# A last layer in row-major form: residual rows by DMA transposes instead of PE transposes, with merged row phases and paired elementwise work

## The chip, the cores and the metric

One core of one Trainium2 chip. The metric is the device time of one execution in microseconds (us). The kernel before takes 478.95 us (median of 3 runs, 478.73 to 479.54). In the profile the engines are PE (TensorE matmul), PEld (its weight load), DVE (VectorE), ACT (ScalarE), POOL (GpSimd) and SP (SyncE, which here only issues DMA). The profiled span runs from the first to the last instruction and is about 1.8 us shorter than the timed execution (476.7 against 478.50 in the profiled run of before, 479.2 against 481.02 in that of the changed kernel).

## The reference

A cross network (DCN v2) with 6 layers, batch 16384, width 416, all tensors bf16:

```python
B, F, D, L = 16384, 26, 16, 6           # Din = F * D = 416
def reference(x0, ws, bs):
    x = x0
    for l in range(L):
        proj = jnp.einsum('bd,de->be', x, ws[l]) + bs[l]
        x = x0 * proj + x
    return x
```

## The kernel before

The batch is cut into 8 groups of 2048 rows; (g, l) is one layer of one group. The kernel holds x transposed: features on the 128 partitions, batch rows along the free dimension, as three blocks of 128 features plus a tail of 32. A job (g, l) has three output tiles of 128 features; each is 12 full matmuls of 512 columns and 4 small ones, then ACT adds the bias out of PSUM, and DVE multiplies by x0 and adds the old x. Jobs of different groups are interleaved, so that PE need not wait for the elementwise work:

```python
order[-6:] = [(5, 5), (7, 3), (6, 4), (7, 4), (6, 5), (7, 5)]     # the last six jobs
...
late = items.index(("tile", (LAST, L - 2), NT - 1))               # (7,4)'s last tile goes last
items.append(items.pop(late))
```

A finished group is turned back into rows by DMA transposes into a staging buffer and stored, all of it on the SP queue, which issues them in the order of the program (in the SP timeline further down at 451.73, 454.33, 456.22 and 464.19 us):

```python
def output(g):
    turn(0)                                   # DMA transpose, 128 features x 2048 rows
    add("sp", ... dma_start_transpose(ot3, x3s[s3]) ...)          # the 32-feature tail
    add("pool", ... tensor_copy(ost[..., 384:416], ot3) ...)
    turn(1); turn(2)
    ... dma_start(rows ..., ost ...)          # the store, 1664 KB
```

The very last job (7,5) is different. It computes rows directly (x as the stationary operand, W as the moving one), so that its output needs no turning at the end. For that the residual x of group 7 (the input of layer 5) must also be in rows. The kernel before turns it on PE, in two row phases that share the PSUM banks with the matmuls:

```python
def turn_main(kp, bks, ts):                   # PE transposes into PSUM
    for j in range(NJ):
        for h2 in range(2):
            for t in ts:
                add("pe", ... h.transpose(psum_t(bks[j])[...], xcol(t, j, kk), ident) ...)

def rows_out(kp, bks):                        # PSUM to SBUF, 832 columns each
    for j in range(NJ):
        eng = "act" if j == 0 or (kp and j == 2) else "dve"
        ...
def nat_mul(kk, j, b):                        # ACT copies 416 columns out of PSUM, DVE multiplies by x0
    ...
def nat_add(kk, j):                           # DVE adds the residual, 416 columns
    ...
turn_main(0, bka, (0, 1)); turn_tails(0, bka); nat_rows(0, bkb, True)
for j in range(NJ): nat_full(0, j, bkb[j], False, (0, 1))
turn_main(0, bka, (2,)); rows_out(0, bka)
layer_full(0, bkb, (2,))
turn_main(1, bka, (0, 1, 2)); turn_tails(1, bka); rows_out(1, bka)
nat_rows(1, bkb, True); layer_full(1, bkb)
nat_store(0, 2, 0, NJ)                        # stores: 832, 416, 208, 104 and 104 KB
nat_rows(2, bka, True); layer_full(2, bka); nat_store(2, 3, 2, NJ)
nat_rows(3, bkb, True); layer_full(3, bkb); nat_store(3, 4, 3, NJ, "act")
```

## Time and profile before

| | before |
|---|---|
| time, median of 3 | 478.95 us |
| span of the profile | 476.7 us |
| last column-major matmul ends | 458.0 us |
| group 6's store issues | 464.19 us |
| DVE's last add ends | 474.47 us |

The page's head and its DMA queue q1 (packets, MB, share of 16 engines' time), for the kernel before:

```profile
span 476.7 us, 8467 instructions
PE 470.2 (99%) x3403; PEld 198.7 (42%) x3403; DVE 406.9 (85%) x714; ACT 342.4 (72%) x371; POOL 7.2 (2%) x14
...
q1 hardware_dynamic: 131064, 51.20, 46.8%
...
PE 92%; SPq 4%; DVE 2%; ACT 1%; DMA 0%; issue 0%
```

The last line is the chain of waits by engine: for 92% of the span the kernel waits for PE. The change concerns only the end, where this average says nothing.

For comparing ends I use a mark: the start of the last group of 16 small 32x32 matmuls, which every kernel of this study has. In the PE timeline of before (start, duration, line, operation, count) it is the first of these lines:

```profile
447.02 0.43 PE L471 MATMUL ps<-x,w 32*32 32x512 bf16 x16
447.25 0.42 PE L488 MATMUL ps<-x,w 32*32 32x512 bf16 x8
```

So the end, from the mark, takes 476.7 - 447.02 = 29.68 us. I call this the tail. The spans are read to 0.1 us here, so a tail is good to 0.05 us.

The DVE timeline of before, its last entries:

```profile
461.69 1.57 DVE L795 COPY x<-ps 128x832 bf16<-128x832 bf16 x3
...
473.48 0.58 DVE L825 TENSOR_TENSOR x<-ps,x 128x416 bf16<-128x416 f32 x1
474.09 0.38 DVE L835 TENSOR_TENSOR x<-x,x 128x416 bf16<-128x416 bf16 x1
```

DVE runs from 461 to 474.47 us with no idle stretch over 0.2 us; the span ends 2.2 us after it, which is the last small store. The SP queue of before (when each DMA is issued):

```profile
451.73 2.20 SPq L636 DMA_TRANSPOSE ost<-x  x1
454.33 1.20 SPq L641 DMA_TRANSPOSE ot<-x  x1
456.22 4.32 SPq L636 DMA_TRANSPOSE ost<-x  x2
464.19 0.38 SPq L655 DMA_DIRECT2D out_dram<-ost  x1
468.96 4.98 SPq L842 DMA_DIRECT2D out_dram<-x  x4
```

Group 6 is turned from 451.7 us on and stored at 464.19. The same stretch as windows (start and end, length, busy time of PE, PEld, DVE, ACT and POOL in this order, granted clock, DMA share, GB/s; the DMA share is the summed time of the packets over 16 engines, so overlapping packets can bring it above 1, as in the 1.17 and 1.10 of the changed kernel further down):

```profile
458.00:465.00 7.00, 6.88 (x95) 4.80 (x93) 7.00 (x20) 4.29 (x8) 0.00 (x0) 1.00 0.85 135
465.00:473.30 8.30, 7.38 (x52) 3.85 (x49) 7.99 (x26) 6.25 (x13) 0.00 (x0) 1.00 1.00 334
473.30:476.70 3.40, 0.00 (x0) 0.00 (x0) 1.13 (x3) 0.00 (x0) 0.00 (x0) 0.97 0.54 188
```

The DMA engines are full from 465 to 473, but only 0.54 busy in the last 3.4 us: they have caught up and wait for DVE. I read from this that the end of the kernel before is DVE's; e3 below supports it.

### The profile page before, as it was taken

Reading aid. Unit: us, or ns where it says so; the run is one execution under the profiler, and the core shown is the slowest. Engines: PE = TensorE matmul, PEld = TensorE weight load, DVE = VectorE, ACT = ScalarE, POOL = GpSimd, SP = SyncE. Lnnn points to the kernel's source line nnn. Section 1 sums busy time; section 2 is a strip of 40 time slices with the busy share of each in tenths; the row PEclk is TensorE's granted clock in tenths of the full one; section 3 lists DMA queues with packets and bytes.
Section 4 is the critical chain, followed back from the end, with each engine's and each line's share of the span. In section 5 each row is a group of like instructions: output and inputs, shape, how many; then the busy total and the mean of one; then the engine's idle time right before and its main releaser. Section 6 shows DMA issues by size and latency. Waiting matters only on the chain.

```text
span 476.7 us, 8467 instructions
## 1 busy us (share of the span) xinstructions
PE 470.2 (99%) x3403; PEld 198.7 (42%) x3403; DVE 406.9 (85%) x714; ACT 342.4 (72%) x371; POOL 7.2 (2%) x14
## 2 busy tenths in 40 slices
PE   8999999999999999999999999999999999999996
PEld 6344444444444444444444444434444444444353
DVE  2888888888888888898888879888888888888897
ACT  4677777777777777777777777777777777777775
POOL 0000000000000000000000000000000000000000
PEclk9999999999999999999999999999999999999999
DMA  8886920720102477379219932970000138026388
GB/s 232 179 176 144 195 66 1 157 65 1 34 1 46 76 212 156 75 168 242 57 35 211 207 80 40 189 236 0 2 15 21 26 64 231 0 45 159 108 145 286
DMA packets 131851, 52.27 MB, mean 110 GB/s; under 512 B 108122, under 2 KB 130404, under 8 KB 131812
## 3 DMA queue, kind: packets, MB, share of 16 engines
q1 hardware_dynamic: 131064, 51.20, 46.8%
q8 instruction: 26, 0.43, 0.4%
q10 hardware_dynamic: 748, 0.54, 0.3%
q14 instruction: 13, 0.11, 0.1%
HBM read 5.97 MB, written 13.63 MB: 41 GB/s over the span
## 4 chain that ended last, share of the span: by engine, by line
PE 92%; SPq 4%; DVE 2%; ACT 1%; DMA 0%; issue 0%
PE ps L456 75%; PE ps L477 7%; PE ps L497 7%; SPq L292 2%; PE ps L800 1%; PE ps L471 1%; DVE x L408 1%; DVE tw L403 1%; SPq L297 1%; PE ps L488 1%; SPq L285 0%; SPq L521 0%; ACT tw L394 0%; PE ps L770 0%; DMA x<-ost 0%; SPq L304 0%
## 5 line engine op out<-in xcount | busy, mean ns | idle before, releaser
L394 ACT ACTIVATE tw<-ps,bias 128x1024 bf16<-128x1024 f32 (+1 forms) x295 | 299.8, 1071 | 120.0 <-PE ps L477 75.9
L456 PE MATMUL ps<-x,wm 128*128 128x512 bf16 x1692 | 379.4, 379 | 0.0
L456 PEld LDWEIGHTS ps<-x,wm 128*128 128x128 bf16 x1692 | 159.0, 98 | 213.2 <-issue 28.3
L403 DVE TENSOR_TENSOR tw<-tw,x 128x1024 bf16<-128x1024 bf16 (+1 forms) x285 | 192.7, 685 | 53.9 <-ACT tw L394 53.6
L408 DVE TENSOR_TENSOR x<-tw,x 128x1024 bf16<-128x1024 bf16 (+1 forms) x285 | 182.5, 681 | 0.0
L477 PE MATMUL ps<-x,w 32*128 32x512 bf16 x512 | 39.2, 379 | 0.2 <-DMA x<-ost 0.2
L497 PE MATMUL ps<-x,wm 128*32 128x512 bf16 x564 | 33.0, 380 | 0.0
L434 ACT ACTIVATE ts<-ps,bias 128x512 bf16<-128x512 f32 x47 | 28.8, 701 | 0.0
L438 DVE TENSOR_TENSOR x<-ts,x 128x512 bf16<-128x512 bf16 x47 | 18.6, 417 | 3.0 <-DMA x<-x 3.0
L497 PEld LDWEIGHTS ps<-x,wm 128*32 128x32 bf16 x564 | 13.8, 96 | 17.6 <-issue 5.3
L477 PEld LDWEIGHTS ps<-x,w 32*128 32x128 bf16 x512 | 7.8, 92 | 27.9 <-issue 27.1
L436 DVE TENSOR_TENSOR ts<-ts,x 128x512 bf16<-128x512 bf16 x47 | 18.6, 418 | 0.0
L643 POOL COPY ost<-ot 128x512 bf16<-128x512 bf16 x7 | 6.3, 900 | 449.9 <-DMA ot<-x 449.9
L800 PE MATMUL ps<-wm,x 128*128 128x416 bf16 x48 | 9.4, 341 | 0.0
L568 DVE COPY x<-ps 128x512 bf16<-128x512 bf16 x4 | 1.7, 425 | 8.0 <-PE ps L561 8.0
L828 ACT ACTIVATE x<-ps 128x416 bf16<-128x416 f32 x15 | 7.1, 525 | 1.3 <-PE ps L800 1.1
L565 ACT ACTIVATE x<-ps 128x512 bf16<-128x512 bf16 x8 | 4.3, 594 | 4.8 <-PE ps L561 4.8
L800 PEld LDWEIGHTS ps<-wm,x 128*128 128x128 bf16 x48 | 5.1, 115 | 3.8 <-issue 1.4
L488 PE MATMUL ps<-x,w 32*32 32x512 bf16 x188 | 5.9, 374 | 0.0
L830 DVE TENSOR_TENSOR x<-x,x 128x416 bf16<-128x416 bf16 x15 | 5.4, 368 | 0.3 <-ACT x L828 0.2
L471 PE MATMUL ps<-x,w 32*32 32x512 bf16 x208 | 5.6, 385 | 0.0
L835 DVE TENSOR_TENSOR x<-x,x 128x416 bf16<-128x416 bf16 x16 | 5.6, 369 | 0.1
(35 smaller groups left out, 43.2 us busy)
## 6 DMA issues: line engine op xcount, KB each, us to landing
out_dram<-ost SPq DMA_DIRECT2D x7, 1664.0 KB, 6.8
x<-in_x_dram SPq DMA_DIRECT2D x7, 416.0 KB, 7.1
x<-x SPq DMA_DIRECT2D x24, 96.0 KB, 2.2
wm<-in_ws_dram SPq DMA_DIRECT2D x5, 312.0 KB, 3.4
x<-x SPq DMA_DIRECT2D x22, 64.0 KB, 2.0
x<-ost SPq DMA_DIRECT2D x28, 32.0 KB, 2.3
out_dram<-x SPq DMA_DIRECT2D x1, 832.0 KB, 4.3
x<-x SPq DMA_DIRECT2D x24, 32.0 KB, 1.9
```

The lines of the kernel that those rows point to most:

```text
L394: add("act", lambda h, a=a, w=w, b0=b0: h.activation(tw[r][:, a * CH:(a + w) * CH], psum[:, b0 * CH:(b0 + w) * CH], ACT_F.Identity, bias=b ...
L403: add("dve", lambda h, a=a, e=e: h.tensor_tensor(tw[r][:, a * CH:e * CH], tw[r][:, a * CH:e * CH], x0s[s0][:, i * GC + a * CH:i * GC + e * ...
L408: add("dve", lambda h, a=a, e=e: h.tensor_tensor(xs[so][:, i * GC + a * CH:i * GC + e * CH], tw[r][:, a * CH:e * CH], src(i, a, e), ALU.ad ...
L434: add("act", lambda h: h.activation(ts[r][:, :], bank(b), ACT_F.Identity, bias=bias[:, 3, l:l + 1], scale=1.0), reads=[("ps", b), "bias"], ...
L436: add("dve", lambda h: h.tensor_tensor(ts[r][:, :], ts[r][:, :], x03, ALU.mult), reads=[("ts", r)] + tok0, writes=[("ts", r)], release=True)
L438: add("dve", lambda h: h.tensor_tensor(x3s[so][:, :], ts[r][:, :], res, ALU.add), reads=[("ts", r)] + rtok, writes=[("x3", so), ("x3", so, ...
L456: add("pe", lambda h, t=t, j=j: h.matmul(bank(banks[j]), wm[l][:, t, ecols], src(t, j, j + 1), start=(first and t == 0), stop=(not first a ...
L471: add("pe", lambda h, q=q, j=j, r=r, c=c, o=o: h.matmul(psum[o, banks[j] * CH:(banks[j] + 1) * CH], w3[l][q, i * P + c * T32:i * P + (c + ...
L477: add("pe", lambda h, q=q, j=j, r=r: h.matmul(bank(banks[j]), w3[l][q, ecols], src[q, :], start=first, stop=not first, tile_position=(r * ...
L488: add("pe", lambda h, l=l, b=b, s3=s3, ri=ri, qi=qi, ro=ro, qo=qo: h.matmul(psum[qo, b * CH:(b + 1) * CH], w3[l][qi, NT * P:D], s3[qi, :], ...
L497: add("pe", lambda h, t=t, j=j, src=src, l=l, b=b, ro=ro, qo=qo: h.matmul(psum[qo, b * CH:(b + 1) * CH], wm[l][:, t, NT * P:D], src(t, j, ...
L800: add("pe", lambda h, t=t: h.matmul(bank(b, n=D), xcol(t, j, kk), wm[l][:, t, :], start=(first and t == 0), stop=(not first and t == NT - 1)),
```

## The change

The intent is to take work off PE and DVE in the end. The residual rows come by DMA transposes; PE transposes and their copies out of PSUM go; the two first row phases are merged, since no banks are needed for transposes; DVE works on pairs of 416 columns; the bias matmuls use 32 rows (of which 31 are zero) instead of one. For the residual to be in time, group 6's last layer moves ahead of group 7's fifth. Rows now lie as blocks of 128, so each store piece is one row of 832 bytes. "Spread" is the copy that puts the turned 32-feature tail into its columns of the staged rows. The excerpt below leaves out smaller parts of the change: group 6's tail is now turned after its three blocks, the last column-major tile leaves PSUM in pairs of 512 columns, and x0's rows and the bias rows are prepared for the new forms.

```diff
-    order[-6:] = [(5, 5), (7, 3), (6, 4), (7, 4), (6, 5), (7, 5)]
   (the order is then ..., (5,5), (6,4), (7,3), (6,5), (7,4), (7,5))
-    where[((LAST - 1, L - 1), 0)] = batches[-1]
+    where[((LAST - 1, L - 1), 1)] = batches[-1]
-    late = items.index(("tile", (LAST, L - 2), NT - 1))
-    items.append(items.pop(late))
 ...
+    def rest_turn(t, j0=0, j1=NJ):                 # the residual, by DMA
+        s = xset[(LAST, L - 1)]
+        add("sp", lambda h: h.dma_start_transpose(
+            x5f[:, j0 * KK:j1 * KK, t * P:(t + 1) * P], xs[s][:, t * GC + j0 * CH:t * GC + j1 * CH]),
+            reads=..., writes=[("x5n", j, t) for j in range(j0, j1)], ...)
 ...
         finish_tile(g, l)
+        if (g, l) == (LAST, L - 2):
+            if i < NT - 1:
+                rest_turn(i)
+            else:
+                rest_turn(i, 0, 2)
+                rest_turn(i, 2, 4)
+                spread(LAST - 1, "act")            # group 6's tail columns, was on POOL
+                rest_spread()
+                store(LAST - 1)                    # group 6's store, now behind the residual
 ...
-    (turn_main, turn_tails, rows_out: gone)
+    nat_rows(first)                                # row phases 0 and 1 together
+    for t in range(NT - 1):
+        for kk, bks in first:
+            for j in range(NJ):
+                nat_full(kk, j, bks[j], False, (t,))
 ...
+        o, x5v = on[:, j:j + 2, kk, :], x5n[:, j:j + 2, kk, :]    # pairs of 416 columns
 ...
+        dst = out[LAST * GC:B, :].rearrange("(j k p) f -> p j k f", j=NJ, k=KK)[:, j0:j1, kk, :]
```

More of the change, by code (lines that the diff above doesn't have):

```diff
@@ L625, in load_last @@
         for j in range(NJ):
-            add("sp", lambda h, j=j: h.dma_start(x0n7[:, j, :, :], perm(rows7, j)),
+            add("sp", lambda h, j=j: h.dma_start(
+                x0n7[:, j, :, :], rows7[j * CH:(j + 1) * CH, :].rearrange("(k p) f -> p k f", k=KK)),
                 writes=(x0_all(sn) + x03_toks(sn) if j == 0 else []) + [("n7", j)], lane="n7", batch=0)
@@ L629, in load_last @@
             add("sp", lambda h, j=j: h.dma_start(brow[j * T32:j * T32 + 1, :], bs[L - 1:L, :]),
-                writes=[("brow", j)] + (["brow"] if j == 0 else []), lane="brow", batch=0)
+                reads=["brow"], writes=[("brow", j)], lane="brow", batch=0)
     def output(g):
@@ L638, in turn, with turn_tail, spread, copy @@
                 reads=[("x", s, t, j) for j in range(NJ)], writes=[("ost", t)], lane="ot", batch=g)
+        def turn_tail():
+            add("sp", lambda h: h.dma_start_transpose(ot3[:, :, :], x3s[s3][:, :]),
+                reads=[("x3", s3)], writes=["ot3"], lane="ot3", batch=g)
         turn(0)
-        add("sp", lambda h: h.dma_start_transpose(ot3[:, :, :], x3s[s3][:, :]),
-            reads=[("x3", s3)], writes=["ot3"], lane="ot3", batch=g)
-        add("pool", lambda h: h.tensor_copy(
-            ost[:, :, NT * P:D].rearrange("p (j k) f -> p j k f", j=NJ),
-            ot3[:, :, :].rearrange("p k (j f) -> p j k f", j=NJ)),
-            reads=["ot3"], writes=[("ost", NT)])
-        turn(1)
-        turn(2)
+        if g < LAST - 1:
+            turn_tail()
+            spread(g, "pool")
+            turn(1)
+            turn(2)
+            store(g)
+        else:
+            turn(1)
+            turn(2)
+            turn_tail()
+            rest_tail()
+        free_x.append(s)
+        free_3.append(s3)
+    def spread(g, eng):
+        dst = ost[:, :, NT * P:D].rearrange("p (j k) f -> p j k f", j=NJ)
+        sp_ = ot3[:, :, :].rearrange("p k (j f) -> p j k f", j=NJ)
+        copy(eng, dst, sp_, reads=["ot3"], writes=[("ost", NT)])
+    def copy(eng, dst, sp_, **kw):
+        if eng == "act":
+            add("act", lambda h: h.activation(dst, sp_, ACT_F.Copy), **kw)
+        else:
+            add(eng, lambda h: h.tensor_copy(dst, sp_), **kw)
+    def store(g):
         rows = out[g * GC:(g + 1) * GC, :]
@@ L658, in output, with rest_tail, rest_spread @@
                 writes=[("out", g, j0)], lane="out", batch=g)
-        free_x.append(s)
-        free_3.append(s3)
+    x5f = x0s[s5][:, 0:XW + CH].rearrange("p (a f) -> p a f", f=D)
+    hold = []
+    def rest_tail():
+        add("pool", lambda h: h.memset(warm[:, :], 0.0), writes=x0_all(s5) + x03_toks(s5) + ["x5 free"])
+        s3 = xtail[(LAST, L - 1)]
+        hold.append(free_x.pop())
+        ot5 = xs[hold[0]][:, 0:CH].rearrange("p (k f) -> p k f", k=KK)
+        add("sp", lambda h: h.dma_start_transpose(ot5, x3s[s3][:, :]),
+            reads=[("x3", s3)], writes=[("x", hold[0], 0, 0)], lane="ot5", batch=0)
+    def rest_spread():
+        n = turn_of(LAST, L - 1)
+        staged = xs[hold[0]][:, 0:CH].rearrange("p (k q f) -> p q k f", k=KK, q=NJ)
+        for j0, j1 in ((0, NJ - n), (NJ - n, NJ)):
+            if j0 < j1:
+                q0 = (j0 + n) % NJ
+                copy("act", x5n[:, j0:j1, :, NT * P:D], staged[:, q0:q0 + j1 - j0, :, :],
+                     reads=[("x", hold[0], 0, 0), "x5 free"], writes=[("x5n", j, NT) for j in range(j0, j1)])
+    def rest_turn(t, j0=0, j1=NJ):
+        s = xset[(LAST, L - 1)]
+        add("sp", lambda h: h.dma_start_transpose(
+            x5f[:, j0 * KK:j1 * KK, t * P:(t + 1) * P], xs[s][:, t * GC + j0 * CH:t * GC + j1 * CH]),
+            reads=[("x", s, t, j) for j in range(j0, j1)] + ["x5 free"],
+            writes=[("x5n", j, t) for j in range(j0, j1)], lane=f"x5_{t}{j0}", batch=0)
     items = []
     where = {(b[min(1, len(b) - 1)], 0): b for b in batches[:-1]}
-    where[((LAST - 1, L - 1), 0)] = batches[-1]
+    where[((LAST - 1, L - 1), 1)] = batches[-1]
     del where[((0, 0), 0)]
@@ L729, in bass_standalone__cross_network_dcn__recsys_kernel @@
     first_job()
+    add("pool", lambda h: h.memset(brow[:, :], 0.0), writes=["brow"])
     for n, it in enumerate(items):
@@ L740, in bass_standalone__cross_network_dcn__recsys_kernel @@
             rows32(g, l, i, banks, False, mode[n] == "F1")
-            evacuate(g, l, i, banks, list(range(NJ)), 2)
+            if (g, l, i) == (LAST, L - 2, 0):
+                evacuate(g, l, i, banks, [0, 1], 1)
+                evacuate(g, l, i, banks, [2, 3], 2)
+            else:
+                evacuate(g, l, i, banks, list(range(NJ)), 2)
         else:
@@ L745, in bass_standalone__cross_network_dcn__recsys_kernel @@
             if n == len(items) - 1:
-                full(g, l, i, banks, False, True, lambda j: evacuate(g, l, i, banks, [j], 1))
+                full(g, l, i, banks, False, True,
+                     lambda j: evacuate(g, l, i, banks, [j - 1, j], 2) if j % 2 else None)
             else:
@@ L750, in bass_standalone__cross_network_dcn__recsys_kernel @@
         finish_tile(g, l)
+        if (g, l) == (LAST, L - 2):
+            if i < NT - 1:
+                rest_turn(i)
+            else:
+                rest_turn(i, 0, 2)
[3 more added lines that the diff above has]
+                store(LAST - 1)
     g, l = LAST, L - 1
@@ L757, in xcol @@
     def xcol(t, j, kk):
-        return src(t, j, j + 1).rearrange("p (m k) -> p m k", k=KK)[:, :, kk]
+        return src(t, j, j + 1)[:, kk * P:(kk + 1) * P]
     def x3col(j, kk):
-        return s3[quad(g, l, j)[1], :].rearrange("p (m k) -> p m k", k=KK)[:, :, kk]
-    first_use = {"x5": True, "on": True}
-    def turn_main(kp, bks, ts):
-        for j in range(NJ):
-            for h2 in range(2):
-                for t in ts:
-                    o = h2 * CH + t * P
-                    add("pe", lambda h, j=j, t=t, kk=2 * kp + h2, o=o: h.transpose(
-                        psum_t(bks[j])[:, o:o + P], xcol(t, j, kk), ident[:, :]),
-                        reads=[stok(t, j), "ident"], writes=[("ps", bks[j])])
-    def turn_tails(kp, bks):
-        for h2 in range(2):
-            for j in range(NJ):
-                r, q = quad(g, l, j)
-                o = h2 * CH + NT * P
-                add("pe", lambda h, j=j, q=q, r=r, kk=2 * kp + h2, o=o: h.matmul(
-                    psum_t(bks[j])[:, o:o + T32], x3col(j, kk), ident[q, q], is_transpose=True,
-                    tile_position=(r * T32, 0)),
-                    reads=tok3 + ["ident"], writes=[("ps", bks[j])])
-    def rows_out(kp, bks):
-        for j in range(NJ):
-            extra = x0_all(s5) + x03_toks(s5) if first_use.pop("x5", None) else []
-            eng = "act" if j == 0 or (kp and j == 2) else "dve"
-            dst = x5n[:, j, 2 * kp:2 * kp + 2, :]
-            sp_ = psum_t(bks[j]).rearrange("p (a f) -> p a f", a=2)[:, :, 0:D]
-            if eng == "act":
-                add("act", lambda h, dst=dst, sp_=sp_: h.activation(dst, sp_, ACT_F.Copy),
-                    reads=[("ps", bks[j])], writes=extra + [("x5n", j, kp)])
-            else:
-                add("dve", lambda h, dst=dst, sp_=sp_: h.tensor_copy(dst, sp_),
-                    reads=[("ps", bks[j])], writes=extra + [("x5n", j, kp)])
+        return s3[quad(g, l, j)[1], kk * P:(kk + 1) * P]
+    first_use = {"on": True}
     def nat_full(kk, j, b, first, ts=range(NT)):
@@ L803, in nat_full, with nat_rows @@
                 reads=[stok(t, j), ("wm", l)], writes=[("ps", b)])
-    def nat_rows(kk, bks, first):
-        for part in range(2):
+    def nat_rows(kks):
+        for kk, bks in kks:
             for j in range(NJ):
                 r, q = quad(g, l, j)
-                st, sp_ = first and part == 0, not first and part == 1
-                if part == 0:
-                    add("pe", lambda h, j=j, q=q, r=r, st=st: h.matmul(
-                        bank(bks[j], n=D), x3col(j, kk), w3[l][q, :], start=st, stop=False,
-                        tile_position=(r * T32, 0)),
-                        reads=tok3 + [("w3", l, r)], writes=[("ps", bks[j])])
-                else:
-                    add("pe", lambda h, j=j, r=r, sp_=sp_: h.matmul(
-                        bank(bks[j], n=D), ones[r * T32:r * T32 + 1, :], brow[r * T32:r * T32 + 1, :],
-                        start=False, stop=sp_, tile_position=(r * T32, 0)),
-                        reads=["ones", ("brow", r)], writes=[("ps", bks[j])])
@@ L821, in nat_mul @@
-    def nat_mul(kk, j, b):
-        extra = x0_all(so) + x03_toks(so) if first_use.pop("on", None) else []
-        o, x0v = on[:, j, kk, :], x0n7[:, j, kk, :]
-        if kk == KK - 1 and j == NJ - 1:
-            add("dve", lambda h: h.tensor_tensor(o, bank(b, n=D), x0v, ALU.mult),
-                reads=[("ps", b), ("n7", j)], writes=extra + [("on", j, kk)])
-        else:
-            add("act", lambda h: h.activation(o, bank(b, n=D), ACT_F.Copy),
-                reads=[("ps", b)], writes=extra + [("on", j, kk)])
-            add("dve", lambda h: h.tensor_tensor(o, o, x0v, ALU.mult),
-                reads=[("on", j, kk), ("n7", j)], writes=[("on", j, kk)])
+                add("pe", lambda h, kk=kk, b=bks[j], j=j, q=q, r=r: h.matmul(
+                    bank(b, n=D), x3col(j, kk), w3[l][q, :], start=True, stop=False, tile_position=(r * T32, 0)),
+                    reads=tok3 + [("w3", l, r)], writes=[("ps", bks[j])])
@@ new lines, in nat_rows, with nat_mul @@
+        for kk, bks in kks:
+            for j in range(NJ):
+                r, q = quad(g, l, j)
+                add("pe", lambda h, b=bks[j], q=q, r=r: h.matmul(
+                    bank(b, n=D), ones[q, :], brow[q, :], start=False, stop=False, tile_position=(r * T32, 0)),
+                    reads=["ones", ("brow", r)], writes=[("ps", bks[j])])
+    def nat_mul(kk, j, bks):
+        extra = x0_all(so) + x03_toks(so) if first_use.pop("on", None) else []
+        for a in (j, j + 1):
+            add("act", lambda h, a=a: h.activation(on[:, a, kk, :], bank(bks[a], n=D), ACT_F.Copy),
+                reads=[("ps", bks[a])], writes=extra + [("on", a, kk)])
+        o, x0v = on[:, j:j + 2, kk, :], x0n7[:, j:j + 2, kk, :]
+        toks = [("on", j, kk), ("on", j + 1, kk)]
+        add("dve", lambda h: h.tensor_tensor(o, o, x0v, ALU.mult),
+            reads=toks + [("n7", j), ("n7", j + 1)], writes=toks)
@@ L833, in nat_add, with nat_store @@
     def nat_add(kk, j):
-        o, x5v = on[:, j, kk, :], x5n[:, j, kk, :]
+        o, x5v = on[:, j:j + 2, kk, :], x5n[:, j:j + 2, kk, :]
+        toks = [("on", j, kk), ("on", j + 1, kk)]
         add("dve", lambda h: h.tensor_tensor(o, o, x5v, ALU.add),
-            reads=[("on", j, kk), ("x5n", j, kk // 2)], writes=[("on", j, kk)])
+            reads=toks + [("x5n", a, t) for a in (j, j + 1) for t in range(NT + 1)], writes=toks)
     stores = [0]
-    def nat_store(k0, k1, j0, j1, eng="sp"):
-        dst = out[LAST * GC:B, :].rearrange("(j p k) f -> p j k f", j=NJ, k=KK)[:, j0:j1, k0:k1, :]
-        add(eng, lambda h: h.dma_start(dst, on[:, j0:j1, k0:k1, :]),
-            reads=[("on", j, kk) for j in range(j0, j1) for kk in range(k0, k1)],
-            writes=[("out7", k0, j0)], lane=f"out7_{stores[0]}", batch=0)
+    def nat_store(kk, j0, j1, eng="sp"):
+        dst = out[LAST * GC:B, :].rearrange("(j k p) f -> p j k f", j=NJ, k=KK)[:, j0:j1, kk, :]
+        add(eng, lambda h: h.dma_start(dst, on[:, j0:j1, kk, :]),
+            reads=[("on", j, kk) for j in range(j0, j1)],
+            writes=[("out7", kk, j0)], lane=f"out7_{stores[0]}", batch=0)
@@ L845, in nat_store @@
         stores[0] += 1
     bka, bkb = take(NJ), take(NJ)
-    last = KK - 1
-    def layer_full(kk, bks, ts=range(NT)):
-        for j in range(NJ):
-            nat_full(kk, j, bks[j], False, ts)
-            nat_mul(kk, j, bks[j])
-            if kk < last:
-                if j:
-                    nat_add(kk, j - 1)
-            elif j == 1:
-                nat_add(kk, 0)
-                nat_add(kk, 1)
-                nat_store(kk - 1, kk + 1, 0, 2)
-            elif j == 2:
-                nat_add(kk, 2)
-                nat_store(kk, kk + 1, 2, 3)
-        nat_add(kk, NJ - 1)
@@ L866, in bass_standalone__cross_network_dcn__recsys_kernel @@
-    turn_main(0, bka, (0, 1))
-    turn_tails(0, bka)
-    nat_rows(0, bkb, True)
-    for j in range(NJ):
-        nat_full(0, j, bkb[j], False, (0, 1))
-    turn_main(0, bka, (2,))
-    rows_out(0, bka)
-    layer_full(0, bkb, (2,))
-    turn_main(1, bka, (0, 1, 2))
-    turn_tails(1, bka)
-    rows_out(1, bka)
-    nat_rows(1, bkb, True)
-    layer_full(1, bkb)
-    nat_store(0, 2, 0, NJ)
-    nat_rows(2, bka, True)
-    layer_full(2, bka)
-    nat_store(2, 3, 2, NJ)
-    nat_rows(3, bkb, True)
@@ L884, in bass_standalone__cross_network_dcn__recsys_kernel @@
-    layer_full(3, bkb)
-    nat_store(3, 4, 3, NJ, "act")
+    first = [(0, bka), (1, bkb)]
+    nat_rows(first)
+    for t in range(NT - 1):
+        for kk, bks in first:
+            for j in range(NJ):
+                nat_full(kk, j, bks[j], False, (t,))
+    for js in ((0, 1), (2, 3)):
+        for kk, bks in first:
+            for j in js:
+                nat_full(kk, j, bks[j], False, (NT - 1,))
+    nat_mul(0, 0, bka)
+    nat_mul(0, 2, bka)
+    nat_mul(1, 0, bkb)
+    nat_add(0, 0)
@@ new lines, in bass_standalone__cross_network_dcn__recsys_kernel @@
+    nat_mul(1, 2, bkb)
+    nat_add(1, 0)
+    nat_add(0, 2)
+    nat_store(0, 0, NJ)
+    nat_add(1, 2)
+    nat_store(1, 0, NJ)
+    for kk, bks in ((2, bka), (3, bkb)):
+        nat_rows([(kk, bks)])
+        for j in range(NJ):
+            nat_full(kk, j, bks[j], False)
+            if j % 2:
+                nat_mul(kk, j - 1, bks)
+                nat_add(kk, j - 1)
+                if kk == KK - 1:
+                    nat_store(kk, j - 1, j + 1, "sp" if j == 1 else "act")
+        if kk < KK - 1:
+            nat_store(kk, 0, NJ)
```

## The prediction

> **What bounds it now.** Span 476.7 us, timed 478.95. The page has PE busy 99%, DVE 85%, ACT 72%; the chain of waits is 92% PE. Only the end changes. Timeline of the end: the last column-major tile leaves PE at 457.9, DVE finishes its residual add at 461.4, row-mode matmuls end about 472.2, DVE's last add at 474.47, the last store about 476.2. There PE runs 48 full matmuls at 187 ns (9.0 us), 32 small ones (2 us) and 64 transposes (about 3.0 us of issue). DVE is the closer limit: no gap over 0.2 us from 461 to 474.
>
> **Removed.** (a) 64 PE transposes: 3.0 us of PE. (b) Eight PSUM-to-SBUF copies of 832 columns: 5 on DVE (2.6 us), 3 on ACT (2.5). (c) Pairing: 31 DVE operations of 416 columns at 0.286 us net become 16 of 832; interpolated from the net times of 512 (0.335) and 1024 columns (0.62) these take 0.51 each: 9.0 to 8.2 us. (d) The GpSimd copy at 457.3, beside which a DVE add took 0.4 us longer[...].
>
> **Added.** Five DMA transposes on the SP queue: about 8 us of issue (2.2 full, 1.2 small or half). Three ACT copies (1.6 us), where ACT now waits. Stores in 832-byte pieces: the present group stores have them and reach 350 GB/s.
>
> **New schedule (estimate).** The order change puts group 6's last layer earlier; tile counts up to 457.9 are unchanged. SP issues group 6's transposes at about 446 to 455, the residual's at 456 to 463; the last land near 465 to 466. PE waits about 0.8 us at 458 for ACT to free the last tile's banks, since no transposes cover that now; matmuls end near 470.3 (before 472.2). DVE's first row-mode add comes about 466.4, just after the residual lands. From there DVE is back to back: thirteen operations, last add near 473 (before 474.5). So most of what is removed is lost to ACT's evacuation (16 copies at 0.44 us) and that late first add.
>
> **The store tail takes part back.** DMA share is about 1.0 from 465 to 473 at 350 GB/s: group 6's store and group 7's share the engines. Group 6's store still cannot issue before 463.5 (behind the residual transposes). 3.33 MB at 350 GB/s from 464.5 is 9.5 us: 474 at best; with the last 208 KB issued at 473 it lands about 475, end about 475.5. [...]
>
> **Prediction:** 477.6 us (0.3% faster), 8 in 10 between 475.8 and 479.5. Faster by over 2%: 0.01; within 2%: 0.97; slower by over 2%: 0.02.
>
> **What would show it.** Right: no PE transposes after 458, row mode ending near 470, DVE's last add near 473, DMA share about 1 from 465 to 475, the span before 450 unchanged within 0.3 us. Wrong if: DVE's first add waits beyond 467 for a transpose (each us late is nearly a us of span); or transposes land by 464 and the store goes early, so the end is 474 or less; or PE waits over 1 us for the last evacuation; or the reordered tiles wait on rotated tails around 447 to 452.
>
> **What would make it wrong.** SBUF-to-SBUF transposes queueing (about 2.4 us of DMA each at 212 GB/s), or the new order slowing the middle.

## The result, and the profile after

The changed kernel takes 480.94 us (median of 6 runs, 480.62 to 481.34) against 479.02 us before (6 runs). The ratio is 1.004, 95% interval 1.0027 to 1.0053: within 2%, and slower, not faster. A ratio here is the mean time of one kernel's fast runs over that of the other's in the same rounds, so it is not quite the ratio of the medians quoted.

The page of the changed kernel, the lines that answer to those of before:

```profile
span 479.2 us, 8276 instructions
PE 461.9 (96%) x3285; PEld 195.0 (41%) x3339; DVE 402.3 (84%) x691; ACT 341.2 (71%) x371; POOL 6.3 (1%) x15
...
q1 hardware_dynamic: 140056, 52.79, 49.1%
...
PE 91%; DVE 2%; DMA 2%; ACT 2%; issue 1%; SPq 0%; ACTq 0%; DVEq 0%
```

DVE has 4.6 us less to do and PE 8.3 us less by the page. Not all of the PE figure is real: 54 matmuls are missing from this trace (1638 of 1692 on the line of the full matmuls). The SP queue has 1.6 MB more to move: 1.7 MB of residual transposes, less 0.1 MB of stores that now go through ACT's queue. The span is 2.5 us longer. The mark:

```profile
448.06 0.43 PE L470 MATMUL ps<-x,w 32*32 32x512 bf16 x16
```

The mark is 1.04 us later than before. The tail is 479.2 - 448.06 = 31.14 us, 1.46 us more than the 29.68 of before. So the longer span has two parts: 1.04 us that were lost before the mark, and 1.46 us in the tail. From the first such group of 16 (28.09 us before, 29.13 after) to the mark it is 418.93 us in both, so the 1.04 us were lost in the first 29 us, where the two programs have the same instructions but for one memset on GpSimd.

DVE in the end:

```profile
460.93 1.28 DVE L407 TENSOR_TENSOR x<-tw,x 128x1024 bf16<-128x1024 bf16 x2
465.27 0.59 DVE L856 TENSOR_TENSOR x<-x,x 128x832 bf16<-128x832 bf16 x1 [3.06 <-ACT x L852]
...
467.42 0.59 DVE L862 TENSOR_TENSOR x<-x,x 128x832 bf16<-128x832 bf16 x1
...
473.93 0.59 DVE L862 TENSOR_TENSOR x<-x,x 128x832 bf16<-128x832 bf16 x1
```

DVE's last add ends at 474.52 us, 26.46 us after the mark, where it was 27.45 before: DVE is 0.99 us earlier. The change did that part of its work. But the span ends 4.7 us after that add, not 2.2. The SP queue of after says where to look:

```profile
446.89 7.69 SPq L636 DMA_TRANSPOSE ost<-x  x3
454.62 1.95 SPq L641 DMA_TRANSPOSE ot<-x  x1
456.61 1.26 SPq L693 DMA_TRANSPOSE x<-x  x1
457.99 8.41 SPq L707 DMA_TRANSPOSE x<-x  x4
466.50 0.53 SPq L678 DMA_DIRECT2D out_dram<-ost  x1
469.54 4.56 SPq L869 DMA_DIRECT2D out_dram<-x  x4
```

The four residual transposes take the queue from 457.99 to 466.40, and group 6's store of 1664 KB stands behind them. It is issued 18.44 us after the mark, where it was 17.17. The windows:

```profile
459.00:467.50 8.50, 7.57 (x55) 3.45 (x55) 4.97 (x10) 5.54 (x12) 0.00 (x0) 1.00 1.17 183
467.50:477.80 10.30, 4.03 (x28) 1.75 (x26) 6.88 (x14) 3.97 (x9) 0.00 (x0) 0.79 1.10 332
```

From 467.5 to 477.8 the DMA engines are full without a break, at 332 GB/s; over three microseconds of that lie after DVE's last add. In the trace's own DMA records the first packet of these stores starts at 467.64 and the last ends at 478.18, 3.41 MB in all. Before, the same bytes went from 465.16 to 475.83, with breaks in which they waited for DVE. One more difference stands in these records. In before, group 7's two larger stores (832 and 416 KB) went out in pieces of 1664 bytes, and where these alone filled the engines (470.5 to 472.0 us) they moved 385 to 389 GB/s (the 334 of the window above averages these with pieces of 832 bytes and with the idle ends of the window). In the changed kernel every piece is 832 bytes, and from 471.0 to 477.5 us they moved 329 to 335. The new layout of the rows thus seems to cost drain time by itself: an estimate from these rates is about half a microsecond (1.28 MB at 332 instead of 388 GB/s). No run here changes the pieces alone, so this share is not shown. From the mark, the stores begin 1.44 us later than before (19.58 against 18.14), and the tail is 1.46 us longer.

### The profile page after: what moved, and what is told of

It is laid out like the page before. It is cut to its first block, busy times and chain, and to the rows that moved or that the text cites. A ratio compares the mean times of both kernels' runs of the same rounds, so it can differ in the third digit from the quotient of the medians.

```text
span 479.2 us, 8276 instructions
## 1 busy us (share of the span) xinstructions
PE 461.9 (96%) x3285; PEld 195.0 (41%) x3339; DVE 402.3 (84%) x691; ACT 341.2 (71%) x371; POOL 6.3 (1%) x15
## 4 chain that ended last, share of the span: by engine, by line
PE 91%; DVE 2%; DMA 2%; ACT 2%; issue 1%; SPq 0%; ACTq 0%; DVEq 0%
PE ps L455 76%; PE ps L476 7%; PE ps L496 6%; ACT tw L393 1%; DMA wm<-in_ws_dram 1%; PE ps L470 1%; DVE x L862 1%; DMA x<-x 1%; PE ps L487 1%; DVE x L856 1%; DVE tw L402 0%; PE ps L560 0%; DVE x L407 0%; SPq L707 0%; ACT x L564 0%
## 5 line engine op out<-in xcount | busy, mean ns | idle before, releaser
L455 PE MATMUL ps<-x,wm 128*128 128x512 bf16 x1638 | 371.9, 379 | 6.6 <-issue 3.8
L669 POOL COPY ost<-ot 128x512 bf16<-128x512 bf16 x6 | 4.9, 809 | 423.3 <-DMA ot<-x 423.3
L856 DVE TENSOR_TENSOR x<-x,x 128x832 bf16<-128x832 bf16 x8 | 4.7, 587 | 3.5 <-ACT x L852 3.5
L560 PE MATMUL ps<-ident,x 128*128 128x128 bf16 x64 | 5.3, 243 | 0.3 <-ACT x L564 0.3
```

The source lines that it names most:

```text
L455: add("pe", lambda h, t=t, j=j: h.matmul(bank(banks[j]), wm[l][:, t, ecols], src(t, j, j + 1), start=(first and t == 0), stop=(not first a ...
```

## The experiments

Theory A: the end is now the DMA engines draining the stores of groups 6 and 7, which begin behind the residual transposes. Rivals: B, DVE's adds wait for a residual that lands late; C, the loss lies in the start. A table of all profiles, each time counted from that profile's own mark:

| run | mark | group 6's store issues | DVE's last add ends | tail | time, median | ratio to before (95%) |
|---|---|---|---|---|---|---|
| before | 447.02 | 17.17 | 27.45 | 29.68 | 478.95 | |
| before_again | 449.68 | 17.12 | 27.44 | 29.72 | 481.16 (one run) | |
| after | 448.06 | 18.44 | 26.46 | 31.14 | 480.94 | 1.0040 (1.0027 to 1.0053) |
| after_again | 446.92 | 18.44 | 26.47 | 31.18 | 480.22 | 1.0022 (1.0006 to 1.0038) |
| e1_half_store6 | 448.31 | 18.45 | 26.46 | 29.09 | 478.79 | 0.9982 (0.9952 to 1.0012) |
| e2_add_without_residual | 447.47 | 18.42 | 26.47 | 31.13 | 480.73 | 1.0029 (1.0004 to 1.0055) |
| e3_order_only | 447.11 | 14.00 | 27.70 | 29.89 | 480.37 | 1.0022 (0.9986 to 1.0058) |
| e4_order_and_pairs | 447.82 | 13.91 | 27.96 | 30.18 | 479.42 | 1.0002 (0.9977 to 1.0026) |
| e5_store6_on_act | 447.61 | 12.78 | 31.97 | 34.59 | 484.94 | 1.0125 (1.0100 to 1.0149) |
| e6_no_residual_dma | 449.49 | 12.77 | 26.47 | 29.01 | 478.69 | 0.9991 (0.9970 to 1.0013) |
| e7_store6_first | 447.14 | 11.89 | 31.45 | 34.06 | 483.25 | 1.0082 (1.0064 to 1.0099) |
| e8_first_block_by_pe | 447.69 | 17.25 | 25.78 | 30.31 | 479.79 | 1.0015 (0.9992 to 1.0038) |
| e9_fetch_moved | 447.99 | 18.64 | 26.47 | 31.41 | 481.27 | 1.0047 (1.0030 to 1.0063) |
| e10_pe_block_fetch_moved | 448.70 | 16.84 | 25.79 | 29.80 | 479.73 | 1.0019 (1.0002 to 1.0036) |

The times of the runs scatter by more than the effect, because the mark does. The tail does not: the two profiles of the same kernel agree within 0.04 us, which is within the reading of the spans. The single run of before_again: only its tail and its mark are used.

### Does the start belong to the change? (before_again, after_again)

No edit: each kernel again, before with one look and after with five rounds.

> The kernel before, unaltered, for a second profile. Theory A: tail time (span's end less the start of the last group of 16 small 32x32 tail matmuls) again 29.5 to 29.9 us, whatever the start did.

> The changed kernel again, unaltered, with five rounds against the kernel before, and a second profile of it. Tail time here is the span's end less the start of the last group of 16 small 32x32 tail matmuls; it was 29.68 us before and 31.14 after. Theory A (the drain): tail 31.0 to 31.3 again, and the start (first full matmul at 6.2 us before, 7.4 after in the first profiles) differs by chance, so slower by 1.4 to 1.9 us. Theory C (the change makes the start slower): the last small tail matmuls again start at 448.0 or later.

The kernel before, unaltered, had its mark at 449.68 us in its second profile, 2.66 us later than in the first; its tail was 29.72. The changed kernel had its mark at 446.92 in its second profile, earlier than any other profile here, and a tail of 31.18. The PE timeline of before_again, in its start, shows where most of this lateness comes from:

```profile
7.46 2.72 PE L456 MATMUL ps<-x,wm 128*128 128x512 bf16 x6 [0.78 <-DMA wm<-in_ws_dram]
```

The first full matmuls waited for the first weights, whose load took 5.92 us in that chain of waits, and then ran slowly; in the first profile of before they started at 6.18 us and took 1.46. So the 1.04 us that the first two profiles differ by ahead of the mark is chance in the start, and theory C is out. What makes the first load late in some executions is open, and it is not all that moves the mark: in e2 the first full matmul started at 6.02 us, earlier than in before, and the mark came at 447.47. In the repeat the changed kernel was slower by 0.22%, in the first comparison by 0.40%; the tail's 1.46 us is 0.30%. The repeat's medians differ by 0.9 us (480.22 against 479.33), less than the 1.4 to 1.9 us expected, so that part of the expectation failed; the tail and the mark were as theory A said.

### Is it the drain or a late residual? (e1, e2)

e1 leaves out half of group 6's last store (a wrong result):

```diff
+        if g == LAST - 1:
+            parts = [("(j k p) f -> p j k f", 0, NJ // 2)]
```

> The changed kernel, but group 6's last store writes only half of its rows (832 KB instead of 1664 KB; a wrong result on purpose). Theory A (the end is the DMA engines draining group 6's and group 7's stores behind the residual transposes): 832 KB less at about 333 GB/s is 2.5 us less, until DVE's last add (474.5) plus the last store's 2.2 us bounds it, so 1.8 to 2.5 us faster than the changed kernel, DVE's end unmoved. Theory B (the end is set by the residual landing late and DVE's adds behind it): no change, within 0.3 us. Theory C (the loss lies at the start): no change in the end, within 0.3 us.

The tail fell from 31.14 to 29.09 us, 2.05 us less, with DVE's last add exactly where it was (26.46). The DMA engines were no longer full after that add; these are e1's windows, the last one beginning where DVE ends:

```profile
467.80:474.80 7.00, 3.98 (x28) 1.71 (x26) 6.84 (x13) 3.93 (x9) 0.00 (x0) 0.95 0.97 313
474.80:477.40 2.60, 0.00 (x0) 0.00 (x0) 0.00 (x0) 0.00 (x0) 0.00 (x0) 0.50 0.44 152
```

e2 lets the adds read x0 in place of the transposed residual. The transposes still run and nothing waits for them. (It is not the right computation; the two inputs are so close that the comparison with the reference passes it.)

```diff
-        o, x5v = on[:, j:j + 2, kk, :], x5n[:, j:j + 2, kk, :]
+        o, x5v = on[:, j:j + 2, kk, :], x0n7[:, j:j + 2, kk, :]
```

> The changed kernel, but the last layer's adds read x0 instead of the transposed residual (a wrong result on purpose): the DMA transposes still run, nothing waits for them. Theory A: DVE's last add comes at most 0.6 us earlier and the span stays within 0.4 us of the changed kernel, because the same bytes drain. Theory B: the adds no longer wait, 0.5 to 1.5 us faster. Theory C: within 0.3 us.

Tail 31.13, DVE's last add at 26.47: nothing moved by more than 0.02 us. DVE's first add in e2 starts 19.36 us after the mark, to the hundredth where it was in the changed kernel (467.42 less 448.06):

```profile
466.83 0.58 DVE L862 TENSOR_TENSOR x<-x,x 128x832 bf16<-128x832 bf16 x1
```

The residual was landing just in time, and waiting for it cost nothing. Theory B is out. The chain of waits of the changed kernel does pass through a residual transpose:

```profile
463.72 3.27 DMA x<-x
466.99 0.03 issue
467.02 0.05 DVEq L167
467.07 0.35 issue
467.42 0.59 DVE x L862
```

That piece is real but not binding: with it removed, DVE was held to the same instant by the multiply before it, which waits for ACT. This is a case in which the chain names a step that costs nothing.

### What the residual transposes cost the drain (e6)

e6 is e2 without the four residual transposes:

```diff
-            if i < NT - 1:
-                rest_turn(i)
-            else:
-                rest_turn(i, 0, 2)
-                rest_turn(i, 2, 4)
+            if i == NT - 1:
                 spread(LAST - 1, "act")
```

> The changed kernel without the four residual transposes of 128 columns; the adds read x0 instead (a wrong result on purpose). Theory A: the store goes out near 461 (after ACT's spread), the stores are drained before DVE is done, DVE's last add keeps its place (26.5 us after the last small tail matmuls), and the end follows it by 2.2 to 2.6 us: tail 28.7 to 29.3, 2 us less than the changed kernel. If the residual transposes do not matter: tail stays at 31.1.

The store issued 12.77 us after the mark instead of 18.44, the tail was 29.01 us, and DVE's last add stayed at 26.47. The windows of e6 show the engines half idle before the end:

```profile
463.00:468.50 5.50, 5.38 (x33) 2.50 (x32) 1.99 (x5) 2.86 (x7) 0.00 (x0) 1.00 0.95 303
468.50:476.00 7.50, 4.46 (x31) 1.99 (x28) 7.32 (x14) 4.40 (x10) 0.00 (x0) 0.96 0.55 181
```

So the transposes on the DMA path cost 31.14 - 29.01 = 2.13 us of tail, by their bytes and by holding back the store together; e6 does not part the two. In e6, as in e1, the span ends about 2.6 us after DVE's last add, with a last store of 208 KB (before: 2.2 us, 104 KB). Even without them, everything else of the change is worth only 29.68 - 29.01 = 0.67 us, about 0.14% of the kernel. That is the most this change could have won with its row phases as they are.

### Can the store simply go earlier? (e5, e7)

If only the store's place in the queue were at fault, issuing it earlier would mend it. e5 issues it from the ACT queue, after ACT's spread:

```diff
                 spread(LAST - 1, "act")
+                store(LAST - 1, "act")
                 rest_spread()
-                store(LAST - 1)
```

> The changed kernel, but group 6's last store is issued from the ACT queue after ACT's spread, so it does not stand behind the residual transposes on the SP queue (correct result). Theory A says the late issue of that store is a large part of the loss: issue near 461 instead of 466.5, the drain ends 0.8 to 1.5 us earlier, tail 29.7 to 30.4. A rival within A, that only the amount of DMA work counts and the engines have no idle time to fill: tail within 0.3 us of 31.1.

I expected 29.7 to 30.4 and got 34.59, the worst of all. The DVE timeline of e5 shows the new wait:

```profile
466.46 0.59 DVE L856 TENSOR_TENSOR x<-x,x 128x832 bf16<-128x832 bf16 x1 [0.23 <-ACT x L852]
472.47 0.59 DVE L862 TENSOR_TENSOR x<-x,x 128x832 bf16<-128x832 bf16 x1 [5.42 <-DMA x<-x]
```

The residual landed about 5 us later. Counted in the DMA records, from 464 to 467 us each quarter of a microsecond started 76 to 91 packets of the SP queue (256 bytes each, the transposes) and 76 to 81 of the ACT queue (832 bytes each, the store). The two queues thus got equal counts of packets, and the transposes about a quarter of the bytes. Nor did the second queue add bandwidth here: the two together moved about 345 GB/s in these 3 us (342 to 349 in e5's windows), no more than one queue alone (349 to 355 GB/s from 439 to 442 us in the kernel before, during group 5's store).

e7 keeps the store on the SP queue, after the first residual transpose, and lets GpSimd do the spread:

```diff
+            if i == 0:
+                rest_turn(i)
+                spread(LAST - 1, "pool")
+                store(LAST - 1)
+            elif i < NT - 1:
+                rest_turn(i)
```

> The changed kernel, but group 6's store is issued on the SP queue after the first residual transpose and before the other three; GpSimd spreads its tail columns (correct result). The store then starts near 460, but its 5 us of DMA work stand in front of the residual. Theory A with the DMA engines as the limit: the wait turns up elsewhere, DVE's first add is released by a transpose 1.5 to 3 us later than 467.4, and the tail is 30.5 to 31.6, no real gain. If only the place of the store mattered: tail 29.2 to 29.7.

The kind of outcome was as expected and the size was not: the first add waited 4.90 us for a transpose, and the tail was 34.06 us, not 30.5 to 31.6. The store of 1664 KB took about 5 us (e7's windows from 461 to 466 us show 315 to 339 GB/s), and all of it went in front of what DVE needs. Between the two ends, "store first" and "residual first", the residual first is by far the better. The loss of the change is therefore not a bad order of the queue alone; it is 1.6 MB of transposes put into a stretch whose DMA engines were needed for 3.4 MB of stores (and, by the estimate above, the smaller pieces of these stores).

### The order and the pairs by themselves (e3, e4)

e3 is the kernel before with the order of the change and nothing else (the first three hunks of the diff above).

> The kernel before with nothing but the new order of the last group-layers (group 6's last layer before group 7's fifth, tails one tile later); PE transposes, single elementwise operations and old stores stay. Theory A: group 6's store goes out near 458 instead of 464 and is drained before group 7's stores begin, but the old kernel's end was set by DVE at 474.5 and a last small store, so 0 to 0.5 us faster than before. A rival that the new order itself costs time (waits on rotated tails): 0.5 to 2 us slower than before.

The store went out 3.2 us earlier (14.00 against 17.17), and the tail was 29.89 us, 0.2 us longer than before and so 0.2 us outside what I expected. An earlier store gained nothing, since DVE ended that kernel. The rival of a costly new order got no support: no wait on rotated tails appeared, and from the first group of small matmuls to the mark it is 418.93 us here too. Its four times scatter from 478.86 to 481.82 us, and the interval of the ratio holds 1.

e4 adds the pairs to e3 for the first three row phases:

```diff
+        for a in (j, j + 1):
+            add("act", ... h.activation(on[:, a, kk, :], bank(bks[a], n=D), ACT_F.Copy) ...)
+        o, x0v = on[:, j:j + 2, kk, :], x0n7[:, j:j + 2, kk, :]
+        add("dve", lambda h: h.tensor_tensor(o, o, x0v, ALU.mult), ...)
```

> The kernel before with the new order and with the multiplies and adds of the first three row phases in pairs (12 operations of 832 columns instead of 24 of 416); PE transposes stay. DVE was the closer of the old end: 24 x 0.286 = 6.9 us become 12 x 0.51 = 6.1 us, so 0.3 to 0.8 us faster than the order alone, if the pairing's later start does not eat it. Against theory A it has no residual DMA transposes, so its stores should not be the end: DMA share below 0.9 just before the last store.

DVE's last add came 0.26 us later than in e3, not 0.3 to 0.8 earlier. A pair has to wait until ACT has copied both halves; the DVE timeline of e4 shows such waits in its row mode, the longest of them this one:

```profile
471.44 0.59 DVE L837 TENSOR_TENSOR x<-x,x 128x832 bf16<-128x832 bf16 x1 [0.47 <-ACT x L833]
```

The four waits of this kind (0.15, 0.23, 0.29 and 0.47 us) sum to 1.14 us and more than eat the 0.8 us that fewer instructions were estimated to save. As expected, the DMA engines were not full near this end (share 0.63 from 473.0 to 475.8 us).

### A mixture (e8)

If DMA work is what costs, part of it can go back to PE, which waits 0.81 us for banks anyway. e8 transposes the first 128 residual columns on PE into two idle banks and copies them once on ACT and once on DVE; the other two blocks stay with DMA.

```diff
+    for half in range(2):
+        for a in range(8):
+            j, kk = (half * 8 + a) // KK, a % KK
+            add("pe", ... h.transpose(psum_b(bka[half])[:, a * P:(a + 1) * P], xcol(0, j, kk), ident) ...)
+    for half, eng in ((0, "act"), (1, "dve")):
+        copy(eng, x5f[:, half * 8:(half + 1) * 8, 0:P], psum_b(bka[half]) ..., ...)
+    first = [(0, bkb), (1, bka)]             # row phase 0 starts in the other four banks
-                rest_turn(i)                 # for tile 0
```

> The changed kernel, but the first 128 residual columns are transposed on PE (16 transposes into two of the banks that wait there anyway, one copy on ACT, one on DVE), and only the other two 128-column blocks by DMA; row phase one starts in the other four banks (correct result). Theory A: SP is free about 2 us earlier, group 6's store issues 2 us earlier, 512 KB of transposes leave the DMA engines, the drain ends about 2 us earlier and DVE's last add bounds the end: tail 29.0 to 29.6 us, 1.5 to 2.1 less than the changed kernel, and 0 to 0.7 less than the kernel before. If DMA work is not the cause: tail 31 or more, since PE, ACT and DVE have more to do.

It is better than the changed kernel by 0.83 us of tail (30.31) and short of what I expected. DVE ended 0.7 us earlier (25.78), but the store's issue came only 1.2 us earlier, not 2: the first of the remaining three could not start before its tile was ready, 11.67 us after the mark (in the changed kernel the four start at 9.93), and the three then took 5.48 us of the queue. Against before it is not faster: ratio 1.0015, and the interval holds 1.

### The stop in the transposes (e9, e10)

In the changed kernel one residual transpose took 3.71 us to issue and the others 1.3 to 1.9 us. In its DMA records, per quarter of a microsecond, the 256-byte packets of the SP queue were:

```
from us    462.00 462.25 462.50 462.75 463.00 463.25 463.50 463.75 464.00
packets       177     93     13      0      3      9      9     58    285
```

At 462.22 us a packet of 16 KB of the kind "instruction" starts on one DMA engine and lasts 0.95 us. The same near stop follows such a packet in other places where transposes are still queued, in both kernels: after the packets at 265.2 us (before) and 266.2 us (after) the counts fall within 0.75 us to 17 or fewer in a quarter of a microsecond, stay there for about 1.25 us and then return to about 280. In the start it is weaker: after the packet at 13.54 us (after) they fall to 20 and no lower. The kernel before has one in its own end too, at 460.3 us. In e3, e4 and e6 no transposes were left to be moved when the packet of their ends came, so those profiles say nothing; in e7 three were queued behind the store, and its windows show 19 GB/s from 467 to 468 us, which is not set against a packet here. In one place where plain copies ran beside it (after, 315.8 us, 832-byte packets) their rate did not change (104 to 116 packets in a quarter of a microsecond from 315 to 318 us); in e5, where the store was queued beside the transposes, 462 to 463 us moved 6 GB/s in all. e9 puts 46 short dummy matmuls at the start in place of 14 longer ones, which moves the fetches of PE's instructions:

```diff
-    keep_busy(14, 7)
+    for _ in range(46):
+        add("pe", lambda h: h.matmul(bank(7, n=16), ones[:, :], ones[:, 0:16], start=True, stop=True), ...)
```

> The changed kernel with 46 short dummy matmuls at the start in place of 14 longer ones, which adds 32 matmul pairs to PE's instruction stream, so that the 16 KB instruction fetch that fell at 14.1 us after the last small tail matmuls in the changed kernel (the first three profiles of it: 14.16, 14.09, 14.14) falls about 5 us earlier, before the second residual transpose is issued (correct result). [...] If the fetch stops them: the quiet at 14.2 to 16 us is gone, the second residual transpose issues in 2.0 to 2.4 us instead of 3.7, group 6's store issues near 17.0 us after the mark instead of 18.4, and as the drain sets the end, the tail is 29.7 to 30.3 instead of 31.15. If the stop has another cause: store at 18.4, tail 31.0 to 31.3.

The fetch moved from 14.16 to 9.25 us after the mark, and the stop moved with it: the second residual transpose now issued in 2.50 us, and the quiet after 14.2 us was gone (e9's windows from 462 to 465 us show 200 to 216 GB/s). But the expectation for the time failed: tail 31.41, store at 18.64. The SP queue of e9:

```profile
456.54 2.30 SPq L695 DMA_TRANSPOSE x<-x  x1
458.95 7.58 SPq L709 DMA_TRANSPOSE x<-x  x4
466.63 0.54 SPq L680 DMA_DIRECT2D out_dram<-ost  x1
```

The four residual transposes took 7.58 us instead of 8.41, and began 1.03 us later after the mark (10.96 against 9.93), because the stop now held up the small transpose ahead of them (2.30 us instead of 1.26). So e9 shows that the stop goes with the fetch; it does not show what the stop costs, since it only moved it from one transpose to another of the same queue.

e10 is e8 with the same dummy matmuls.

> The version with the first residual block transposed on PE, with the same 32 added matmul pairs (correct result). If the fetch stops the transposes: group 6's store issues near 15.8 us after the mark instead of 17.25, tail 29.0 to 29.6 instead of 30.31, at or below the 29.7 of the kernel before. If not: tail 30.2 to 30.5.

Here the stop again held up the small transpose (2.24 us instead of 1.26), but the next one had to wait for its tile anyway (it starts 11.67 us after the mark, as in e8), and it helped: store at 16.84, tail 29.80, half a microsecond better than e8, though not the 29.0 to 29.6 I expected, as 3.41 MB at about 332 GB/s (330 to 334 in e10's windows from 467 to 477 us) behind the last transposes still take over 10 us. This is level with the kernel before (29.68 and 29.72). In time it is not ahead: 479.73 us, ratio 1.0019 (1.0002 to 1.0036). No version with a right result beats the kernel before. The half microsecond is the only measure here of what the stop costs; the tail of the change was 1.46 us longer.

## Why the prediction was wrong

It was right that the change would move the time by far less than 2%, and wrong in the sign: 0.3% faster was predicted, 0.2 to 0.4% slower was measured, and the median of 480.94 us lies above the range's upper end of 479.5. Times below are shifted by the chance 1.04 us of the start where they are compared with the prediction's absolute times.

- **The middle is unchanged:** right; 418.93 us between the first and the last group of small matmuls in both.
- **PE:** right. The wait for banks was 0.81 us (predicted 0.8). The matmuls ended at 471.5 us, 470.5 without the shift (predicted 470.3).
- **DVE's first add:** right in its time: 467.42 us, 466.4 without the shift (predicted 466.4). The prediction put it just after the residual's landing; e2 shows that the multiply ahead of it held it to the same instant, so that both agree is in part luck.
- **DVE's last add:** nearly right. 473.5 without the shift (predicted 473), because at the end each add follows the multiply that it depends on, and such a pair then takes 1.13 us from start to start (the last two adds start at 472.80 and 473.93) instead of twice 0.51.
- **The GpSimd copy:** right. Beside it a pair of DVE adds took 1.70 us before; with the copy moved to ACT the pair took 1.29 us in the end of the changed kernel, and the copy that remains on GpSimd at 433.65 has such a slower pair beside it too (1.70 us at 433.98).
- **The store tail: this is the step that failed.** The prediction had the right mechanism ("the store tail takes part back") and mis-sized two terms of its sum, the time at which the stores can start and the time that they take. By its sum they drain from 464.5 to 474, and the end is not theirs: it comes at 475.5, from the last small store behind DVE. Measured, without the shift, they drain from 466.60 to 477.14, and the end at 478.2 is theirs.
  - *The start, 2.1 us late.* "Group 6's store still cannot issue before 463.5" was a floor and was used as the time; the store issued at 466.50, which is 465.46 without the shift. The five residual transposes began about when predicted (456.61, 455.57 without the shift; predicted 456) but held the SP queue for 9.8 us, until 466.40, where the prediction had them done by 463 and its own sum of issue times was 8. The largest part is the second one, which issued in 3.71 us instead of the 2.2 allowed (the other of its size took 1.93), with the stop after an instruction fetch in it. Moving that stop to the small transpose (e9) did not bring the store forward.
  - *The length, 1.0 us too short.* The stores took 10.54 us and not 9.5: two stores of 1664 KB are 3.41 MB and not 3.33 (0.2 us), and the full stretch moved 332 GB/s and not 350 (0.5 us); the rest is its slower beginning and end. The 350 fits the kernel before from 465.5 to 473 us, but there the pieces of 1664 bytes at 385 to 389 GB/s raised the mean; pieces of 832 bytes begin at about 350 and fall to about 330.
  - Together they put the last packet 3.1 us later than the 474 of the prediction. Of that, 1.5 us were slack before its end, and the measured end follows the last packet by another 1.0 us: so 478.2 instead of 475.5. e1, e2 and e6 show that this drain, and nothing on PE, ACT or DVE, sets the end. None of the four signs under "Wrong if" names it.
- **The start** was not in the prediction. The mark moved by up to 2.8 us between profiles, from before to before_again mostly with the landing of the first weights and the pace of the first matmuls (the first six full ones start at 6.18 us and take 1.46 in before, 7.46 and 2.72 in before_again), and makes up the rest of the difference between the first two profiles.

What stays open: why the first load is late in some executions, why transposes nearly stop beside an instruction fetch, why the rate of 832-byte pieces falls from about 350 to 330 GB/s, and how much of the tail the smaller pieces cost.

## What to carry to other kernels

Moving work from a busy engine to the DMA engines was not free at the end of this kernel, where 3.41 MB still had to be written out: it cost 2.13 us of tail (e6). Count the bytes that must leave after the last compute, and see at which time the DMA engines can start on them and in pieces of which size (here 385 to 389 GB/s where pieces of 1664 bytes went alone, 329 to 335 with pieces of 832). Before moving a store ahead of a load or a transpose, or to another queue, ask what the transfer behind it feeds; here that turned a loss of 1.5 us of tail into one of 4.4 to 4.9. For effects below the scatter of the start, measure from a mark inside the program; two profiles of one kernel then agreed within 0.04 us where whole times differed by over 2 us.

## What else the traces show

- DMA transposes moved 210 to 218 GB/s in the end of the kernel before (453 to 455 us, and 215 from 458 to 459), 212 to 216 in that of the changed kernel (459.5 to 461 us), and there 283 to 290 GB/s in the two microseconds after the stop (464 to 466 us) and also 283 from 452 to 453 us.
- In the profile of the kernel before, a PE transpose of 128x128 is recorded with 219 ns; but they overlap, and 24 in a row took 1.50 us, 62 ns each. For a row of transposes this pace is what counts.
- The start scatters: the first weights of 312 KB landed 4.1 us after their issue in before and 5.9 us in after and before_again, and the mark at 447 us moved by 2.8 us between profiles of programs with nearly the same start.
